# Attention decode kernel: scores computed transposed into PSUM quadrants, with one full-width exp per piece

## The chip, the core and the metric

The kernel runs on one core of a Trainium2 chip. The metric is the time of one execution on the device, in microseconds. The median of the kernel before is 693.8 us. Each time is that of whole executions; the traces are of one profiled execution each. "Before" and "the changed kernel" are the two kernels. A "group" is eight tiles of 128 keys (1024 keys), the unit in which the kernels work, and there are 64 groups in a head. A "head" is one of the 8 key/value heads, each shared by 4 query heads.

The views of the profile that are quoted: the page's groups (instructions by line, engine, operation and shape), the windows (busy time of each engine in stretches of time), the timeline, the DMA queues, and the chain of waits. Engines: PE is the tensor engine, PEld its weight loads, DVE the vector engine, ACT the scalar engine, POOL GpSimd, SP the engine that issues the large DMA transfers.

## The reference

One token goes through an adaLN block with grouped-query attention against a long cache, then a SwiGLU feed-forward block. What takes the time is the attention:

```python
# x: (1, 1, 512), k_cache and v_cache: (1, 8, 65536, 128), all bfloat16
q = (h @ wq).reshape(B, 1, 32, 128).transpose(0, 2, 1, 3)
k = jnp.repeat(k_cache, 4, axis=1)
v = jnp.repeat(v_cache, 4, axis=1)
scores = jnp.einsum('bhqd,bhkd->bhqk', q, k) * 128 ** (-0.5)
p = softmax(scores, axis=-1)
o = jnp.einsum('bhqk,bhkd->bhqd', p, v)
```

The two caches are 2 x 8 x 65536 x 128 x 2 bytes = 268.4 MB. Each byte is read once. The weights add 17 MB.

## The kernel before

All operations go through a small scheduler that puts in the semaphore waits; each engine runs its own operations in program order. The parts that the change and the argument touch (cuts are marked):

```python
NKB = 4; NVB = 4        # K and V buffers of one chunk (2 MB = 8 groups) each
RT = 8; NB = 3; DT = 3  # ring of transposed K; PSUM banks; T runs 3 groups ahead
LV = OPH + LAT          # PV runs 64 + 8 groups behind the scores

dma("sp", "ld_x", xT_bf, x_col, ...)   # 512 pieces of 2 bytes
dma("sp", "ld_c", cT_bf, c_col, ...)   # 512 pieces of 2 bytes
dma("sp", "ld_wmod", ...)              # 3 MB, then wq (4 MB), then K chunks
# ... adaLN, layer norm, q ... then per group o:
def T_op(o):     # PE: 4 transposes of 128x128 fp32 (pairs of bf16) into a PSUM bank
def evac_op(o):  # DVE (ACT for every fourth): that bank -> ring[o % RT]
def S_op(o):
    for pi_ in range(4):
        pair = ring[r][...].rearrange("p (s two) -> p s two", two=2)
        for par in range(2):
            e.matmul(sps[:, sbank, REP*tl:REP*tl + 64], lhsT=pair[:, :, par],
                     rhs=M64[:, g, par, :, :], start=(par == 0), stop=(par == 1))
def bank_ops(o):                        # each 8 groups
    e.tensor_reduce(out=pm4[:, :, k], in_=hview, axis=AX.X, op=ALU.max)   # DVE
    e.tensor_copy(S_sb[gp][:, :, k*BLT:(k+1)*BLT], hview)                 # DVE
def head_softmax_ops(g):                # ACT, 2 pieces x 4 query heads
    e.activation(out=P_sb[gp][:, t0:t1, h], in_=S_sb[gp][:, h, t0:t1], func=ACT.Exp, ...)
def PVU_op(u):                          # each 2 groups: 4 quadrant matmuls
    for j in range(4):
        e.matmul(ops_[32*j:32*j+16, g % 2, 0:512], lhsT=P_sb[...],
                 rhs=vnat[b][:, tl0+4*j:tl0+4*j+4, :], tile_position=(0, 32*j))
# ...
for s in range(NKO + LV):               # main loop, software pipelined
    T_op(s + DT); pump_dma(); evac_op(s + DT)
    S_op(s); ...                        # bank_ops, head_softmax_ops
    PVU_op((s - LV) // 2); pump_dma()   # every second s
```

`pump_dma` issues the next K or V chunk when its buffer's last reader has been issued; the transfer then waits for that reader. In `S_op` the transposed K is the stationary operand, so the scores come out with 128 keys on 128 partitions and 4 query heads along the columns.

## Time and profile before

| | |
|---|---|
| median | 693.8 us (693.62 to 693.9, 4 runs) |
| bytes moved | 286.56 MB |
| rate in the middle of the run | 426 to 427 GB/s |
| PE, DVE, ACT busy in the 80 us of one head | 65 to 69, 40 to 42, 20 to 21 us |

The windows of the kernel before. The columns are: stretch, its length, busy time of each engine with the number of instructions, granted clock, mean busy share of the 16 DMA engines, GB/s.

```profile
...
core 0: us, PE busy (x) PEld busy (x) DVE busy (x) ACT busy (x) POOL busy (x), PEclk, DMA share, GB/s
0.00:20.00 20.00, 3.87 (x100) 3.65 (x100) 3.41 (x17) 1.49 (x2) 4.36 (x24) 1.00 0.79 316
...
40.00:52.00 12.00, 12.00 (x207) 11.81 (x206) 10.33 (x19) 4.86 (x5) 0.00 (x0) 1.00 1.01 424
52.00:70.00 18.00, 18.00 (x310) 17.71 (x309) 15.56 (x26) 6.25 (x7) 0.00 (x0) 1.00 0.99 409
...
420.00:500.00 80.00, 66.32 (x926) 54.56 (x926) 42.00 (x71) 20.39 (x31) 0.48 (x1) 0.96 1.01 427
...
645.00:670.00 25.00, 10.04 (x74) 3.90 (x74) 1.53 (x5) 0.00 (x0) 0.00 (x0) 0.50 0.96 356
...
```

The row 420:500 is one head; the others between 100 and 580 us read the same. The DMA engines are busy all the time and deliver 427 GB/s, while every compute engine has idle time. At 52 to 70 us, where K comes alone because no probabilities exist yet for V, PE is busy without a gap and the rate is 409 GB/s. The start (0:20) and the weights at the end (645:670) are slower.

The groups of the kernel before: busy time in us, mean ns of one, and idle time of the engine before them.

```profile
...
L491 PE MATMUL sps<-M,arena_k 128*128 128x64 bf16 x4096 | 211.6, 197 | 0.0
...
L558 PE MATMUL ops<-arena_v,P_sb 128*16 128x512 bf16 x1024 | 106.5, 428 | 31.7 <-DMA arena_v<-in_A_v_cache_dram 31.4
L525 ACT ACTIVATE P_sb<-S_sb,negm 128x448 bf16<-128x448 f32 x32 | 36.4, 1289 | 0.0
L503 DVE TENSOR_REDUCE pm<-sps 128x4 f32<-128x256 f32 x64 | 26.6, 416 | 2.0 <-PE sps L491 2.0
L510 DVE COPY S_sb<-sps 128x256 f32<-128x256 f32 x64 | 26.5, 414 | 0.0
...
L525 ACT ACTIVATE P_sb<-S_sb,negm 128x64 bf16<-128x64 f32 x32 | 11.5, 428 | 0.3
...
```

Exp takes 1289 ns for 448 columns and 428 ns for 64: 861 ns for 384 columns, or 2.24 ns per column.

The DMA queues of the kernel before (packets, MB, share of the time of 16 engines), and the chain of waits that ended last:

```profile
...
q1 hardware_dynamic: 27528, 285.49, 98.2%
q8 instruction: 61, 1.00, 0.6%
...
```

```profile
...
DMA 70%; PE 23%; SPq 4%; DVE 2%; issue 0%
...
```

Queue q8 is not data: it is the fetch of instructions, by its kind. The table counts its 61 packets against the same 16 DMA engines as K and V. The start of the kernel before, from its timeline:

```profile
...
0.72 0.43 SPq L283 DMA_DIRECT2D xT_bf<-in_A_x_dram  x1
...
1.21 0.49 SPq L283 DMA_DIRECT2D cT_bf<-in_c_dram  x1
...
1.75 0.50 SPq L284 DMA_DIRECT2D arena_v<-in_w_mod_dram  x1
...
5.95 0.17 DVE L362 TENSOR_SCALAR sc_d<-cT_bf 128x4 f32<-128x4 bf16 x1 [4.02 <-DMA cT_bf<-in_c_dram]
...
29.53 3.68 PE L448 MATMUL ktp<-identf,arena_k 128*128 128x128 f32 x16 [0.80 <-DMA arena_k<-in_A_k_cache_dram]
...
```

### The profile page before, as it was taken

How to read it: one execution, taken by the hardware profiler on the slowest of the kernel's cores; microseconds unless marked ns; L12 is line 12 of the kernel's file. 1: busy time of each engine (PE TensorE's matmuls, PEld its weight loads, DVE VectorE, ACT ScalarE, POOL GpSimd, SP SyncE). 2: the span in 40 equal slices, each digit the busy share in tenths (PEclk: the TensorE clock that was granted, in tenths of full speed). 3: DMA queues.
4: the chain of work that ended last, by engine and by line, in shares of the span. 5: the costliest groups of instructions: out<-in, count | busy, mean ns of one | idle time of the engine just before them, and what ended most of it. 6: DMA issues, size and time to landing. Idle time of an engine off the chain costs nothing.

```text
span 691.6 us, 16865 instructions
## 1 busy us (share of the span) xinstructions
PE 543.6 (79%) x7781; PEld 448.5 (65%) x7781; DVE 333.6 (48%) x594; ACT 167.0 (24%) x253; POOL 8.8 (1%) x33
## 2 busy tenths in 40 slices
PE   1599998788887897888988788788887887784345
PEld 1599986666666676677767676666776776661024
DVE  1288865456444554455645545455553564450001
ACT  0033522142112421214212412114211422123000
POOL 2000000000000000000000000000000000000000
PEclk9999999999999999998989999999998999995555
DMA  7999999999999999999999999999999999999996
GB/s 300 427 428 409 422 427 424 426 428 422 430 426 424 428 427 425 427 425 427 425 427 427 426 423 428 427 425 427 425 425 427 425 428 426 425 410 415 417 329 230
DMA packets 27598, 286.56 MB, mean 414 GB/s; under 512 B 3208, under 2 KB 9096, under 8 KB 10632
## 3 DMA queue, kind: packets, MB, share of 16 engines
q1 hardware_dynamic: 27528, 285.49, 98.2%
q8 instruction: 61, 1.00, 0.6%
q14 instruction: 9, 0.07, 0.0%
HBM read 285.48 MB, written 0.00 MB: 413 GB/s over the span
## 4 chain that ended last, share of the span: by engine, by line
DMA 70%; PE 23%; SPq 4%; DVE 2%; issue 0%
DMA arena_k<-in_A_k_cache_dram 44%; DMA arena_v<-in_A_v_cache_dram 24%; PE ktp L448 13%; PE sps L491 5%; SPq L284 4%; PE ops L558 3%; DMA arena_k<-in_B_w_down_dram 3%; DVE arena_k L474 1%; PE misc L573 1%; DVE X_sb L567 1%; DVE pm L503 0%; DVE S_sb L510 0%; PE misc L674 0%; SPq L283 0%; PE misc L515 0%
## 5 line engine op out<-in xcount | busy, mean ns | idle before, releaser
L448 PE MATMUL ktp<-identf,arena_k 128*128 128x128 f32 x2048 | 349.1, 296 | 69.6 <-DMA arena_k<-in_A_k_cache_dram 69.6
L474 DVE COPY arena_k<-ktp 128x512 f32<-128x512 f32 x398 | 275.0, 691 | 258.4 <-PE ktp L448 256.3
L448 PEld LDWEIGHTS ktp<-identf,arena_k 128*128 128x128 f32 x2048 | 229.6, 148 | 126.5 <-issue 67.8
L476 ACT ACTIVATE arena_k<-ktp 128x1024 bf16<-128x1024 bf16 x114 | 116.7, 1024 | 444.1 <-PE ktp L448 444.1
L491 PE MATMUL sps<-M,arena_k 128*128 128x64 bf16 x4096 | 211.6, 197 | 0.0
L491 PEld LDWEIGHTS sps<-M,arena_k 128*128 128x128 bf16 x4096 | 198.8, 101 | 8.2 <-issue 0.2
L558 PE MATMUL ops<-arena_v,P_sb 128*16 128x512 bf16 x1024 | 106.5, 428 | 31.7 <-DMA arena_v<-in_A_v_cache_dram 31.4
L558 PEld LDWEIGHTS ops<-arena_v,P_sb 128*16 128x16 bf16 x1024 | 24.6, 89 | 57.0 <-DMA arena_v<-in_A_v_cache_dram 40.4
L525 ACT ACTIVATE P_sb<-S_sb,negm 128x64 bf16<-128x64 f32 (+1 forms) x64 | 47.1, 858 | 0.3
L503 DVE TENSOR_REDUCE pm<-sps 128x4 f32<-128x256 f32 x64 | 26.6, 416 | 2.0 <-PE sps L491 2.0
L510 DVE COPY S_sb<-sps 128x256 f32<-128x256 f32 x64 | 26.5, 414 | 0.0
L567 DVE COPY X_sb<-ops 128x512 f32<-128x512 f32 x8 | 5.5, 683 | 39.6 <-PE ops L558 39.6
L573 PE MATMUL misc<-sel,X_sb 128*128 128x4 f32 x64 | 9.8, 276 | 11.1 <-DVE X_sb L567 11.1
L573 PEld LDWEIGHTS misc<-sel,X_sb 128*128 128x128 f32 x64 | 9.2, 222 | 14.1 <-issue 5.5
L525 ACT ACTIVATION_READ_ACCUMULATOR P_sb<-S_sb,negm 128x1 f32 x64 | 14.2, 222 | 0.0
L660 ACT ACTIVATE g_e<-g_c 128x14 f32<-128x14 f32 x1 | 0.2, 215 | 56.4 <-DVE g_c L658 56.4
L378 PE MATMUL misc<-sT,arena_v 128*128 128x1 bf16 x96 | 2.7, 165 | 13.5 <-DMA arena_v<-in_w_mod_dram 13.5
L508 POOL CROSS_LANE_REDUCE rmax<-pmax 128x4 f32<-128x4 f32 x8 | 3.9, 484 | 598.9 <-PE sps L491 383.7
L378 PEld LDWEIGHTS misc<-sT,arena_v 128*128 128x128 bf16 x96 | 2.6, 104 | 13.5 <-DMA arena_v<-in_w_mod_dram 13.5
L418 PE MATMUL misc<-hT,arena_v 128*128 128x1 bf16 x128 | 3.6, 165 | 6.2 <-DMA arena_v<-in_A_wq_dram 6.2
L635 PE MATMUL misc<-attnT,arena_k 128*128 128x1 bf16 x128 | 3.6, 165 | 5.7 <-DMA arena_k<-in_A_wo_dram 5.7
L418 PEld LDWEIGHTS misc<-hT,arena_v 128*128 128x128 bf16 x128 | 3.5, 104 | 6.3 <-DMA arena_v<-in_A_wq_dram 6.3
(85 smaller groups left out, 44.9 us busy)
## 6 DMA issues: line engine op xcount, KB each, us to landing
arena_k<-in_A_k_cache_dram SPq DMA_DIRECT2D x64, 2048.0 KB, 31.0
arena_v<-in_A_v_cache_dram SPq DMA_DIRECT2D x64, 2048.0 KB, 31.0
arena_v<-in_A_wq_dram SPq DMA_DIRECT2D x1, 4096.0 KB, 22.3
arena_k<-in_A_wo_dram SPq DMA_DIRECT2D x1, 4096.0 KB, 28.6
arena_v<-in_w_mod_dram SPq DMA_DIRECT2D x1, 3072.0 KB, 11.7
arena_k<-in_B_w_gate_dram SPq DMA_DIRECT2D x1, 1792.0 KB, 32.9
arena_k<-in_B_w_up_dram SPq DMA_DIRECT2D x1, 1792.0 KB, 14.8
arena_k<-in_B_w_down_dram SPq DMA_DIRECT2D x1, 1792.0 KB, 18.2
```

Of the source, the lines that this page charges most:

```text
L284: return [e.dma_start(out_ap, in_ap)]
L418: insts.append(e.matmul(misc[:, 64 + hd:64 + hd + 1], lhsT=wq_sb[:, kt, hd * P:(hd + 1) * P], rhs=hT[:, kt:kt + 1], start=(kt == 0), stop= ...
L448: insts.append(e.transpose(ktp[:, bank, pi_ * P:(pi_ + 1) * P], knat32[b][:, j * 4 + pi_, :], identf[:, :]))
L474: emit = lambda e: [e.tensor_copy(ring32[r], ktp[:, bank, :])]
L476: emit = lambda e: [e.activation(out=ring[r], in_=ktp[:, bank, :].bitcast(BF16), func=ACT.Copy)]
L491: insts.append(e.matmul(sps[:, sbank, REP * tl:REP * tl + 8 * 2 * REP], lhsT=pair[:, :, par], rhs=M64[:, g, par, :, :], start=(par == 0), ...
L503: op("dve", f"bmax{bl}", lambda e: [e.tensor_reduce(out=pm4[:, :, k], in_=hview, axis=AX.X, op=ALU.max)], reads=[("sps", sbank)], writes=[ ...
L510: op("dve", f"bcopy{bl}", lambda e: [e.tensor_copy(S_sb[gp][:, :, k * BLT:(k + 1) * BLT], hview)], reads=[("sps", sbank)], writes=[("S", g ...
L525: return [e.activation(out=P_sb[gp][:, t0:t1, h], in_=S_sb[gp][:, h, t0:t1], func=ACT.Exp, bias=negm[gp][:, h:h + 1], scale=SCALE, accum_o ...
L558: insts.append(e.matmul(ops_[32 * j:32 * j + 16, g % 2, 0:512], lhsT=lhsT, rhs=vnat[b][:, tl0 + 4 * j:tl0 + 4 * j + 4, :], start=first, st ...
L567: op("dve", f"xcopy{g}", lambda e: [e.tensor_copy(X_sb[:, :], ops_[:, g % 2, :])], reads=[("ops", g % 2)], writes=[("X",)])
L573: insts.append(e.matmul(misc[:, 8:8 + REP], lhsT=X_sb[:, tau * P:(tau + 1) * P], rhs=sel[:, tau, :], start=(tau == 0), stop=(tau == 3)))
```

## The change

Intent: make the small query operand the stationary one and stream the transposed K, so that scores come out transposed (query heads on partitions, keys along columns). Four PSUM quadrants hold 8 rows each. A unit of 4 groups then needs 8 matmuls of 512 columns in place of 32 of 64, and exp runs over all heads at once: two ACT instructions per head, with 1024 and 7168 columns, in place of eight. The price: only 32 of 128 partitions carry scores, so exp covers four times the columns; and the probabilities must be turned back for the PV matmul, with a DVE transpose and a compacting copy for every two groups. The PV matmuls are issued in two halves, two quadrants each. In passing, the x and c loads move from the SP to the ACT queue.

```diff
-        dma("sp", "ld_x", xT_bf[:, :], x_col, ...)
-        dma("sp", "ld_c", cT_bf[:, :], c_col, ...)
+        dma("act", "ld_c", cT_bf[:, :], c_col, ...)
+        dma("act", "ld_x", xT_bf[:, :], x_col, ...)
 ...
-        def S_op(o): ...
+        def SU_op(u):                     # each 4 groups
+                for a0 in (0, 2):
+                    for par in range(2):
+                        for a in (a0, a0 + 1):
+                            e.matmul(sps[32*a:32*a + 2*REP, sbank, 0:512], lhsT=M8[:, g, par, :],
+                                     rhs=R4[:, :, 32*a:32*a + 32, par], ..., tile_position=(0, 32*a))
+            op("act", f"scopy{u}", ... S_st[gp][:, uh*512:(uh+1)*512] <- sps[:, sbank, :], func=ACT.Copy)
+        def smax_op(u):                   # DVE, two groups later
+            e.tensor_reduce(out=pmu[:, uh:uh+1], in_=S_st[gp][:, uh*512:(uh+1)*512], axis=AX.X, op=ALU.max)
 ...
-                for h in range(REP):
-                        e.activation(out=P_sb[gp][:, t0:t1, h], in_=S_sb[gp][:, h, t0:t1], func=ACT.Exp, ...)
+                    reg = S_st[gp][:, u0*512:u1*512]
+                    e.activation(out=reg, in_=reg, func=ACT.Exp, bias=negm_p[gp][:, 0:1], scale=SCALE, ...)
+        def PT_op(u):                     # DVE, each 2 groups
+            e.transpose(out=PTraw[wb], in_=S_st[gp][:, wh*256:(wh+1)*256])
+            e.tensor_copy(PT[gp][:, wh*64:(wh+1)*64], PTraw[wb] 8 of every 32 columns)
 ...
-            op("pe", f"PVU{u}", emit, ...)                 # 4 quadrants together
+            if half == 0:
+                op("pe", f"PVU{u}a", lambda e: emit(e, (0, 1)), ...)
+                return
+            op("pe", f"PVU{u}b", lambda e: emit(e, (2, 3)), ...)   # one group later
```

(Cuts marked with "..."; also cut are the mask that picks each head's maximum, zeroing of the score banks, and which fourth evacuation goes to ACT.)

## The prediction

> **What bounds the kernel now.** DMA. The timeline in 40 slices shows DMA at 9 in every slice but the first two-tenths of start-up and 422 to 428 GB/s in nearly all; the windows by head (80 us each, from 100 to 580 us) give DMA share 1.01 and 426 to 427 GB/s, while PE is busy 65 to 69 us of 80, DVE 40 to 42, ACT 20 to 21. The chain of waits is 70% DMA. 286.56 MB at 427 GB/s are 671 us; the other 20 us are start-up (first 20 us at DMA share 0.79) and the tail (645 to 670 us at 356 GB/s, then about 4 us of chain after the last weight lands). The change moves no byte of K, V or weights.
>
> **What the change removes and adds, per head (80 us, 64 groups of eight K tiles).**
> - PE: score matmuls go from 512 with 128-column weights (0.40 us per group, 25.6 us) to 128 of 512 columns in quadrants. Four quadrant PV matmuls of 512 columns take 0.39 us together in the timeline, 1.88 us for 16 at half clock, so a unit of eight in pairs is, as an estimate, 0.9 to 1.7 us per four groups: 14 to 27 us. PE gets lighter or stays.
> - ACT: exp loses 8 instructions (4 x 1.29 and 4 x 0.43 us, plus read-outs, about 7.7 us). It gains 16 copies of 512 columns; the 1024-column copy took 1.02 us, so about 0.6 us each, 9.6 us. The new exp covers 8192 columns, because only 32 of 128 partitions hold scores: four times the columns of before. The old exp cost 2.24 ns per column (1289-428 ns over 384), with a strided bf16 output. The new output is contiguous; the Trainium skill ("ScalarE: Activation LUTs", "What ACT_TABLE_LOAD costs") gives 0.833 ns per element for every function, and the 1024-column copy agrees. So 1.1 + 6.2 = 7.3 us. ACT about 30 of 80 us.
> - DVE: loses 8 x (0.416 + 0.414) = 6.6 us. It gains 16 maxima of 512 columns (416 ns for 256 columns, so about 0.68, 11 us), 32 transposes of 256 columns (estimate 0.42 us at the copy's rate; 13.5 us) and 32 small copies (0.2 us; 6.4 us). DVE about 66 of 80 us, the new busiest engine, still under the DMA's pace.
>
> **New waits.** The score copy after the long exp waits for it on ACT, and the maximum of that unit blocks DVE, so evacuations and transposes stall about 4 to 6 us once per head. K/V loads take 31 us from issue to landing at 4.9 us a chunk, so about six are in flight; the stall thins that queue and doesn't drain it.
>
> **What reaches the critical path.** The x and c loads leave the SP queue, so the first large load issues at about 0.7 instead of 1.75 us: 1 us gained. At 52 to 70 us, where only K streams, PE was 100% busy and DMA fell to 409 GB/s; there DVE (0.52+0.17 us per group) now takes PE's place: from 1 us gained to 1.5 lost. The tail is V and weight DMA; extra small operations hide under the 5.7 us wait for wo.
>
> **Prediction: 692.8 us, 690.5 to 697.0.** Faster by over 2%: 0.01; within 2%: 0.94; slower by over 2%: 0.05.
>
> **Right if** the windows per head still show 425 GB/s or more, with DVE 60 to 70, PE under 65, ACT 27 to 33 of 80 us; the groups show the 7168-column exp near 6.2 us and the transpose near 0.4. **Wrong if** the transposes or exp run at 2 ns per column or slower: then DVE or ACT stalls drain the load queue, DMA share falls below 0.97 in mid-kernel and the time goes to 710 or more.

## More of the kernel before

The c load lands before 6 us, and the first K transpose runs at 29.53 us, as soon as K is there.

## The result, and the profile after

The changed kernel has a median of 691.07 us (690.22 to 692.11, 9 runs) against 693.83 us (13 runs of before). The ratio is 0.9959, 95% interval 0.995 to 0.9969. Ratios here are the mean time of one kernel's fast runs over that of the other's fast runs of the same rounds, so not quite the ratio of the medians that are quoted. The gain of 2.8 us is small but clear of noise. Later the same kernel gave 692.13 us and 0.9976 (after_again, below).

The windows of the changed kernel, for the stretches shown of before and with the same columns:

```profile
...
0.00:20.00 20.00, 2.70 (x96) 2.64 (x96) 2.79 (x9) 1.49 (x2) 5.38 (x32) 1.00 0.92 339
...
40.00:52.00 12.00, 12.00 (x113) 8.04 (x111) 11.49 (x20) 7.54 (x10) 0.00 (x0) 1.00 0.96 371
52.00:70.00 18.00, 18.00 (x168) 12.55 (x167) 17.10 (x29) 11.25 (x14) 0.00 (x0) 1.00 1.00 404
...
420.00:500.00 80.00, 72.51 (x539) 38.28 (x537) 62.91 (x141) 32.27 (x36) 0.48 (x1) 0.94 1.01 427
...
645.00:670.00 25.00, 8.91 (x66) 3.55 (x58) 2.29 (x9) 0.00 (x0) 0.00 (x0) 0.50 1.02 374
...
```

In the row of one head, DMA still runs at 427 GB/s. DVE went from 42 to 63 us, and PE went up instead of down, from 66 to 73 us. At 40 to 52 us there is a hole that before did not have: 371 GB/s with DMA share 0.96.

The groups that are new or changed:

```profile
...
L590 PE MATMUL ops<-arena_v,PT 128*16 128x512 bf16 x1024 | 193.6, 426 | 54.6 <-DVE PT L566 40.5 <-DMA arena_v<-in_A_v_cache_dram 10.8 <-DVE PTraw L564 3.1
...
L564 DVE STREAM_TRANSPOSE PTraw<-S_st 128x256 bf16<-128x256 bf16 x256 | 111.3, 435 | 1.4 <-ACT S_st L547 1.4
L524 DVE TENSOR_REDUCE pmu<-S_st 128x1 f32<-128x512 bf16 x128 | 86.6, 677 | 40.0 <-ACT S_st L517 40.0
L512 PE MATMUL sps<-arena_k,M 128*8 128x512 bf16 x1024 | 83.0, 395 | 0.3 <-DVE arena_k L486 0.3
L517 ACT ACTIVATE S_st<-sps 128x512 bf16<-128x512 f32 x128 | 75.5, 595 | 54.5 <-PE sps L512 52.3
L547 ACT ACTIVATE S_st<-S_st,negm_p 128x7168 bf16<-128x7168 bf16 x8 | 50.0, 6253 | 0.0
L566 DVE COPY PT<-PTraw 128x64 bf16<-128x64 bf16 x256 | 46.8, 183 | 8.9
...
```

The one long exp takes 6253 ns for 7168 columns. The score matmuls fell from 211.6 to 83.0 us, and the PV matmuls went from 106.5 to 193.6 us although they are the same 1024 matmuls.

The DMA queues and the chain of waits of the changed kernel:

```profile
...
q8 instruction: 37, 0.61, 0.4%
q14 instruction: 14, 0.11, 0.0%
...
```

```profile
...
PE 50%; DMA 25%; DVE 10%; ACT 10%; SPq 4%; issue 1%; POOL 0%; ACTq 0%; DVEq 0%
...
```

The instruction queue q8 carries 37 packets in place of 61. (A second one, q14, carries 14 smaller ones, 8 KB each, in place of 9.) The chain now names PE first with 50%, though the DMA engines are as busy as before. The experiments show what to make of that.

The start of the changed kernel, from its timeline:

```profile
...
0.72 0.48 ACTq L290 DMA_DIRECT2D cT_bf<-in_c_dram  x1
...
0.73 0.45 SPq L291 DMA_DIRECT2D arena_v<-in_w_mod_dram  x1
...
1.23 0.59 ACTq L290 DMA_DIRECT2D xT_bf<-in_A_x_dram  x1
...
13.00 0.17 DVE L379 TENSOR_SCALAR sc_d<-cT_bf 128x4 f32<-128x4 bf16 x1 [5.64 <-DMA cT_bf<-in_c_dram]
...
25.09 0.17 DVE L389 CAST xT<-xT_bf 128x4 f32<-128x4 bf16 x1 [11.07 <-DMA xT_bf<-in_A_x_dram]
...
32.90 3.44 PE L460 MATMUL ktp<-identf,arena_k 128*128 128x128 f32 x15
...
```

The first large load is issued at 0.73 instead of 1.75 us. But c is used only at 13.00 us and x at 25.09 us, since they land that late. The layer norm, q and the first K transpose wait for them, and K starts at 32.90 instead of 29.53 us.

To see where time is gained and lost, take every data packet of the trace and ask when the first N megabytes had landed. The table gives the lag behind the kernel before, in us; negative is ahead. (The bytes of K, V and weights are the same in all of these kernels, and x and c add 2 KB, so equal N is equal progress. This table is worked out from the traces' packets, for one profiled execution each; that of the changed kernel took 690.26 us, near the fast end of its runs. Times count from the start of the trace; counted from the start of the span, a whole column shifts by up to 0.4 us, while the differences down a column stay.)

| MB landed | changed | changed, again | small loads back | before, small loads moved | more waits on PE | rows |
|---|---|---|---|---|---|---|
| 5 | -1.22 | -1.37 | 0.13 | -1.61 | -0.01 | -2.30 |
| 14 | -1.05 | -1.28 | 0.19 | -1.51 | 0.01 | -2.43 |
| 24 | 1.12 | 2.31 | -0.02 | 1.28 | -0.10 | -2.39 |
| 34 | 0.17 | 1.65 | -0.84 | 1.17 | -0.96 | -3.46 |
| 60 | 0.10 | 1.44 | -1.05 | 1.33 | -0.84 | -3.50 |
| 250 | -1.23 | 0.07 | -2.33 | 1.30 | -1.54 | -4.77 |
| 285.4 | -3.34 | -1.82 | -3.78 | 1.69 | -2.22 | -6.32 |

For the changed kernel the column reads: 1.1 us ahead after the start, 2.2 us lost between 14 and 24 MB (about 40 to 65 us), 1.0 us regained by 34 MB, then a slow, steady gain of 1.3 us up to 250 MB, then 2.1 us at the end. In the second profiled execution (692.13 us) the loss between 14 and 24 MB is 3.6 us and the other parts are similar. So a small net result is the sum of several parts; of these the prediction had named the first and, as a range around zero, the one in the phase where K comes alone.

### The profile page after: what moved, and what is told of

The parts are those of the page before. It is cut to its first block, busy times and chain, and to the rows that moved or that the text cites. A ratio compares the mean times of both kernels' runs of the same rounds, so it can differ in the third digit from the quotient of the medians.

```text
span 688.5 us, 11328 instructions
## 1 busy us (share of the span) xinstructions
PE 570.4 (83%) x4709; PEld 315.5 (46%) x4709; DVE 497.9 (72%) x1132; ACT 253.3 (37%) x277; POOL 10.4 (2%) x42
## 4 chain that ended last, share of the span: by engine, by line
PE 50%; DMA 25%; DVE 10%; ACT 10%; SPq 4%; issue 1%; POOL 0%; ACTq 0%; DVEq 0%
PE ktp L460 29%; DMA arena_k<-in_A_k_cache_dram 15%; PE ops L590 11%; ACT S_st L547 9%; PE sps L512 7%; DMA arena_v<-in_A_v_cache_dram 4%; DVE arena_k L486 4%; SPq L291 4%; DMA xT_bf<-in_A_x_dram 3%; DMA arena_k<-in_B_w_down_dram 3%; DVE PTraw L564 2%; PE misc L606 2%; DVE pmu L524 2%; ACT S_st L517 1%; DVE PT L566 1%
## 5 line engine op out<-in xcount | busy, mean ns | idle before, releaser
L460 PE MATMUL ktp<-identf,arena_k 128*128 128x128 f32 x2048 | 339.2, 294 | 15.0 <-DMA arena_k<-in_A_k_cache_dram 8.0
L590 PE MATMUL ops<-arena_v,PT 128*16 128x512 bf16 x1024 | 193.6, 426 | 54.6 <-DVE PT L566 40.5
L488 ACT ACTIVATE arena_k<-ktp 128x1024 bf16<-128x1024 bf16 x114 | 116.8, 1024 | 276.9 <-PE ktp L460 276.9
L524 DVE TENSOR_REDUCE pmu<-S_st 128x1 f32<-128x512 bf16 x128 | 86.6, 677 | 40.0 <-ACT S_st L517 40.0
L564 DVE STREAM_TRANSPOSE PTraw<-S_st 128x256 bf16<-128x256 bf16 x256 | 111.3, 435 | 1.4 <-ACT S_st L547 1.4
L590 PEld LDWEIGHTS ops<-arena_v,PT 128*16 128x16 bf16 x1024 | 43.3, 89 | 143.1 <-DVE PT L566 49.9
L517 ACT ACTIVATE S_st<-sps 128x512 bf16<-128x512 f32 x128 | 75.5, 595 | 54.5 <-PE sps L512 52.3
L512 PE MATMUL sps<-arena_k,M 128*8 128x512 bf16 x1024 | 83.0, 395 | 0.3 <-DVE arena_k L486 0.3
L547 ACT ACTIVATE S_st<-S_st,negm_p 128x1024 bf16<-128x1024 bf16 (+1 forms) x16 | 59.2, 3701 | 33.4 <-DVE negm_p L542 33.4
L566 DVE COPY PT<-PTraw 128x64 bf16<-128x64 bf16 x256 | 46.8, 183 | 8.9
L512 PEld LDWEIGHTS sps<-arena_k,M 128*8 128x8 bf16 x1024 | 13.7, 83 | 22.7 <-issue 22.3
L606 PEld LDWEIGHTS misc<-sel,X_sb 128*128 128x128 f32 x64 | 14.2, 327 | 11.3 <-DVE X_sb L600 11.3
## 6 DMA issues: line engine op xcount, KB each, us to landing
arena_k<-in_A_k_cache_dram SPq DMA_DIRECT2D x64, 2048.0 KB, 25.2
arena_v<-in_w_mod_dram SPq DMA_DIRECT2D x1, 3072.0 KB, 11.3
```

The source lines that it names most:

```text
L460: insts.append(e.transpose(ktp[:, bank, pi_ * P:(pi_ + 1) * P], knat32[b][:, j * 4 + pi_, :], identf[:, :]))
L488: emit = lambda e: [e.activation(out=ring[r], in_=ktp[:, bank, :].bitcast(BF16), func=ACT.Copy)]
L512: insts.append(e.matmul(sps[32 * a:32 * a + 2 * REP, sbank, 0:512], lhsT=M8[:, g, par, :], rhs=R4[:, :, 32 * a:32 * a + 32, par], start=(p ...
L517: op("act", f"scopy{u}", lambda e: [e.activation(out=S_st[gp][:, uh * 512:(uh + 1) * 512], in_=sps[:, sbank, :], func=ACT.Copy)], reads=[( ...
L524: op("dve", f"smax{u}", lambda e: [e.tensor_reduce(out=pmu[:, uh:uh + 1], in_=S_st[gp][:, uh * 512:(uh + 1) * 512], axis=AX.X, op=ALU.max) ...
L547: return [e.activation(out=reg, in_=reg, func=ACT.Exp, bias=negm_p[gp][:, 0:1], scale=SCALE, accum_out=lpart[:, g, pi:pi + 1])]
```

## The experiments

Twelve kernels ran, on three chips, each beside fresh runs of the kernel before (medians 693.64, 693.54 and 693.77 us). All twelve gave correct results.

| run | median us | range us | ratio to before, 95% interval |
|---|---|---|---|
| after_again | 692.13 | 690.83 to 692.78 | 0.9976 (0.9964 to 0.9988) |
| small_loads_back | 690.13 | 689.98 to 690.18 | 0.9949 (0.9937 to 0.9961) |
| before_small_loads_moved | 697.07 | 695.27 to 698.54 | 1.005 (1.0038 to 1.0062) |
| after_more_instructions | 749.51 | 748.14 to 750.08 | 1.0802 (1.0789 to 1.0816) |
| more_waits_on_pe | 690.70 | 690.64 to 690.98 | 0.996 (0.9947 to 0.9972) |
| more_waits_on_pe_double | 797.05 | 796.22 to 798.58 | 1.1492 (1.1475 to 1.1509) |
| pv_whole | 690.00 | 689.91 to 690.1 | 0.9949 (0.9936 to 0.9961) |
| long_stall_1 | 722.61 | 721.0 to 723.51 | 1.0421 (1.0403 to 1.0438) |
| long_stall_2 | 770.61 | 770.1 to 771.16 | 1.1109 (1.1092 to 1.1126) |
| long_stall_1_pv_whole | 690.45 | 690.31 to 690.83 | 0.9954 (0.9939 to 0.9969) |
| rows | 687.36 | 687.2 to 687.42 | 0.991 (0.9897 to 0.9924) |
| rows_pv_whole | 687.25 | 687.1 to 687.55 | 0.9907 (0.9892 to 0.9922) |

### 1. The start: is moving the small loads a gain?

The changed kernel as it is, as a yardstick:

> The changed kernel as it is, so that the other runs of this call have a yardstick from the same chip. Expected: 0.996 of the kernel before (about 691.0 us), within 0.1%.

It gave 692.13 us, 1 us more than expected, with a spread of 2 us.

Then the part undone:

```diff
-        dma("act", "ld_c", cT_bf[:, :], c_col, ...)
-        dma("act", "ld_x", xT_bf[:, :], x_col, ...)
+        dma("sp", "ld_x", xT_bf[:, :], x_col, ...)
+        dma("sp", "ld_c", cT_bf[:, :], c_col, ...)
```

> The changed kernel with the x and c loads back on the SP queue ahead of the large ones, as before the change. Theory (start-up is a trade): the early issue of the large loads brings data 1.1 us sooner, but x and c then land at 13 and 25 us instead of 3.5 and 6 us, the first K transpose starts at 32.9 instead of 29.5 us, K buffers come free later and the load rate falls to 371 GB/s at 40 to 52 us, which costs about 2.2 us of load time. So this run should start K near 29.5 us, keep 420 GB/s or more at 40 to 52 us and be 0.5 to 1.5 us FASTER than the changed kernel (689.5 to 690.5 us). Rival (the early issue is a plain gain, as the prediction said): 1 us SLOWER than the changed kernel, about 692 us.

And the part alone, in the kernel before (the reverse edit):

> The kernel before, with that part of the change alone: x and c loads on the ACT queue. Trade theory: K starts about 3.4 us later, the load rate dips at 40 to 55 us, and since this kernel's K-only phase is slower (0.70 against 0.65 us per group of eight tiles) the lost time isn't regained: 0.5 to 2 us SLOWER than the kernel before (694.3 to 696). Rival (plain gain): 1 us faster, 692.8 us.

The rows of the windows of small_loads_back, then of before_small_loads_moved:

```profile
...
40.00:52.00 12.00, 12.00 (x113) 8.04 (x112) 11.49 (x20) 7.58 (x10) 0.00 (x0) 1.00 1.00 423
52.00:70.00 18.00, 18.00 (x168) 12.50 (x166) 17.11 (x29) 11.25 (x14) 0.00 (x0) 1.00 1.01 430
...
```

```profile
...
40.00:52.00 12.00, 12.00 (x213) 11.81 (x210) 10.33 (x18) 4.47 (x5) 0.00 (x0) 1.00 0.99 376
52.00:70.00 18.00, 18.00 (x311) 17.72 (x308) 15.56 (x26) 6.14 (x6) 0.00 (x0) 1.00 0.98 375
...
```

With the small loads back on SP, K starts at 29.45 us, the hole is gone (423 and 430 GB/s), and the kernel is 2.0 us faster than the changed kernel of the same call (0.5 to 1.5 us had been expected). The part alone makes the kernel before 3.4 us slower by the medians, more than the 0.5 to 2 us that was expected, with 376 and 375 GB/s in these rows. Both directions agree: the rival, a plain gain of 1 us, falls. How a late start becomes a hole shows in the waits of the SP queue: until the first transposes are done, no K buffer comes free for the next load. SP waits up to 11.3 us for the transposes at this point in the changed kernel and up to 7.4 us in small_loads_back (`--waits --engine SP --window 25:70`). The spread is telling as well: the kernels that load x and c as 2-byte pieces on the ACT queue vary by 1.9 to 3.3 us from run to run. With the pieces on SP, small_loads_back varies by 0.2 us, and the kernel before by 0.6 to 1.0 us.

Why do the small loads land late? The Trainium skill ("DMA: Bandwidth & Descriptors", "Queues, rings and completion order") says that SP and ACT each own one row of rings on the same 16 DMA engines, and that an engine takes turns between the rows that have work, packet by packet. On SP the small loads stand ahead of the large ones in the same ring; on ACT they take turns with them. The trace agrees: the 1024 pieces of 2 bytes, 64 per engine, spread over 20.6 us. Those of c came 0.28 us apart on an engine, beside 6 KB packets that took 0.28 us on average, and those of x 0.36 us apart, beside 8 KB packets that took 0.31 us. A piece itself takes 0.009 us.

### 2. Removing the cause instead of moving it

```diff
-        dma("act", "ld_c", cT_bf[:, :], c_col, ...)      # 512 pieces of 2 bytes, x the same
+        dma("act", "ld_c", c_rows[:, :], c_row, ...)     # 4 rows of 256 bytes, x the same
+        op("pe", "cx_tr", lambda e: [
+            e.matmul(misc[:, 300:304], lhsT=c_rows[:, :], rhs=ident[0:4, 0:4], start=True, stop=True),
+            e.matmul(misc[:, 304:308], lhsT=x_rows[:, :], rhs=ident[0:4, 0:4], start=True, stop=True)], ...)
+        # two small DVE copies: misc -> cT_bf, xT_bf
```

> The changed kernel with x and c loaded as 4 rows of 256 bytes on the ACT queue (8 packets in all) and turned by two small matmuls, in place of 1024 packets of 2 bytes. Theory: it keeps the early issue of the large loads (1.1 us) and loses the late landing: x and c land before 5 us, K starts at 28.5 to 29 us, no dip at 40 to 52 us; 1 to 1.8 us faster than with the loads back on SP: 688.3 to 689.2. Rival (the late landing was not what cost time): no better than 690.1.

The windows of rows:

```profile
...
0.00:20.00 20.00, 4.08 (x102) 3.77 (x102) 4.65 (x22) 1.49 (x2) 5.93 (x33) 1.00 0.92 366
...
40.00:52.00 12.00, 12.00 (x114) 8.34 (x114) 11.36 (x19) 7.67 (x10) 0.00 (x0) 1.00 1.02 431
52.00:70.00 18.00, 18.00 (x169) 12.46 (x167) 17.11 (x29) 11.34 (x14) 0.00 (x0) 1.00 1.00 425
...
```

It gave 687.36 us, 6.2 us faster than before and better than expected. K starts at 27.21 us. The start is 2.3 us ahead of before (366 against 316 GB/s in the first 20 us) instead of 1.1 us: the pieces of 2 bytes cost not only their own landing, but also time on the DMA engines for the others. The packets show where: in both the changed kernel and rows the first packet of the 3 MB load starts 1.8 us into the span, but its last packet ends at 11.6 us in the changed kernel and at 10.6 us in rows. So 1.0 of the further 1.2 us is lost while the pieces take turns with that load. The gain over small_loads_back is 2.8 us (1 to 1.8 us had been expected); the run shows it for the whole edit.

### 3. The steady gain: instruction fetch

Between 60 and 250 MB the changed kernel gains 1.3 us at an even pace. The Trainium skill ("Runtime: NRT & Kernel Launch", "Instruction fetch mechanics") says that a sequencer streams its instructions in blocks of 16 KB, which is 256 instructions, through its own DMA queue. The trace agrees to the packet for q8, if that queue serves PE alone: before, 2 x 7781 PE and PEld instructions are 60.8 blocks, and q8 shows 61; in the changed kernel 2 x 4709 are 36.8, and q8 shows 37. A 16 KB instruction packet takes 1.06 us of one engine, so 24 fewer, spread over 16 engines, are an estimated 1.6 us of DMA time over the whole run. Of these packets 40 start between 60 and 250 MB in before and 24 in the changed kernel: 16 fewer, an estimated 1.06 us of the 1.3. The page calls the cost of such a boundary "mostly hidden".

The first test put memsets on POOL:

```diff
+            op("pool", f"fill{s}", lambda e, s=s: [e.memset(scr[:, s*22+i_:s*22+i_+1], 0) for i_ in range(22)], ...)
```

> The changed kernel with 11264 one-byte memsets more on the otherwise idle POOL engine. Fetch theory: the steady gain of about 1.3 us between 160 and 600 us of the changed kernel comes from 5537 fewer instructions, whose fetch takes DMA time (61 against 37 packets of 16 KB, 1.07 us each, over 16 engines: 1.6 us less). 11264 more should bring about 44 more packets and cost 2.5 to 3.5 us against the changed kernel: about 694 us. Rival (the gain comes from the lighter PE or the quicker engines, the fetch is hidden): no change, within 0.5 us.

It came to 749.51 us instead of 694. The memsets were fetched, but through the other queue: q8 stayed at 37, while q14 rose from 14 to 102 packets, 88 more of 8 KB, one for each 128 memsets. What that cost can't be read off, since the memsets slowed the compute. Its queue and its groups:

```profile
...
q14 instruction: 102, 0.84, 0.3%
...
L487 DVE COPY arena_k<-ktp 128x512 f32<-128x512 f32 x398 | 326.9, 912 | 74.1 <-PE ktp L461 67.4
...
L567 DVE COPY PT<-PTraw 128x64 bf16<-128x64 bf16 x256 | 170.3, 665 | 9.8
...
```

The compacting copies went from 183 to 665 ns and the evacuations from 690 to 912 ns, while the transposes stayed near their 435 ns (458). The Trainium skill ("SBUF — State Buffer", "SBUF: two separate sides") says that POOL and some DVE operations take an exclusive lock on a shared port pair; the run agrees that POOL work that shares no data with DVE slows it. That the lock is the cause is not shown. An idle engine was not a free place.

The second test put satisfied semaphore waits into the PE stream, on the base of small_loads_back:

```diff
+                op("pe", f"fill{s}", lambda e: [e.wait_ge(eng_sem["dve"], 1) for _ in range(11)])
```

> Base of this call: the changed kernel with the x and c loads back on SP (690.1 us). This run adds 5632 satisfied semaphore waits to the PE instruction stream, about as many instructions as the change took away (5537)[...]. Fetch theory: about 22 more instruction packets of 16 KB and 1.2 to 1.8 us more than the base: 691.3 to 692. Rival (fetch is hidden; the steady gain comes from lighter engines): 690.1, within 0.3 us.

The instruction queue of more_waits_on_pe:

```profile
...
q8 instruction: 48, 0.79, 0.5%
...
```

It gave 690.70 us, less than the 691.3 to 692 us that were expected: 0.57 us more than its base, and 0.70 us more than pv_whole (below), which is as fast as the base. The profile counts 2801 more instructions and not 5632, and 11 more packets, an estimated 11 x 1.06 / 16 = 0.73 us. In the table above it falls behind small_loads_back by 0.58 us between 60 and 250 MB, with its groups running at the same 4.08 us per four in mid-head. In that stretch it has 8 packets more (31 against 23), so by its own slope the 16 of the change are 0.58 / 8 x 16 = 1.2 us, close to the 1.3 us to be explained. But the dose is not clean: between 34 and 60 MB it loses 0.3 us with no packet more, and after 250 MB another 0.8 us with 1 more (379 against 407 GB/s at 612 to 627 us). So the waits cost time in some other way too, and part of the 0.58 us may be of that kind.

> The earlier run put 5632 waits into the source, but the profile counts only 2801 more instructions than its base and 11 more instruction packets (48 against 37); it cost 0.57 us. This run doubles the dose: about 5600 more instructions, as many as the change took away, 22 more packets. Fetch theory: the cost doubles, 1.0 to 1.4 us against the base with the x and c loads back on SP (690.1): 691.1 to 691.5. Rival (the 0.57 us was something else about these waits): no clear doubling.

This came to 797.05 us. The packets were there (59), but so many waits slow PE itself, so that the load rate falls to 360 GB/s on average. It can't tell fetch from PE time and doubles nothing. Further support comes from the other kernels: before and before_small_loads_moved have the same 61 packets, and their distance stays put between 60 and 250 MB (1.33 and 1.30). The runs with 37 packets gain 1.3 to 1.4 us there, whether PE is busier (changed) or lighter (pv_whole, 1.3 us). So the lighter or busier PE is not the cause, and fetch is the best explanation of the steady gain. It is supported by one dose of half the size that has side effects, and it is not proven: in all these kernels the packets change together with the rest of the attention code.

### 4. Why PE got busier, and whether it matters

```diff
-            if half == 0:
-                op("pe", f"PVU{u}a", lambda e: emit(e, (0, 1)), ...); return
-            op("pe", f"PVU{u}b", lambda e: emit(e, (2, 3)), ...)
+            if half == 0:
+                op("pe", f"PVU{u}", lambda e: emit(e), ...); return      # all four quadrants
```

> Base as above, with the four quadrant PV matmuls of a unit issued together again instead of two and two. Theory: the prediction missed that halves don't overlap as four do (0.39 us for two, 0.39 us for four), which is why PE busy is 71 to 73 of 80 us per head and not under 65. PE busy should fall by 8 to 13 us per head; the time stays within 0.5 us of 690.1 because DMA binds. Rival: PE is a co-limit (it was 50% of the chain of waits), and the time falls by 1 us or more.

The windows of pv_whole for one head, and its PV group:

```profile
...
420.00:500.00 80.00, 60.68 (x542) 36.44 (x538) 61.12 (x142) 32.22 (x36) 0.48 (x1) 0.94 1.01 427
...
```

```profile
...
L590 PE MATMUL ops<-arena_v,PT 128*16 128x512 bf16 x1024 | 110.3, 436 | 81.0 <-DVE PT L566 51.2 <-DMA arena_v<-in_A_v_cache_dram 26.5 <-DVE arena_k L486 2.7
...
```

PE falls to 61 us in this head (61 to 63 in the six that were read), PV matmuls to 110.3 us, and the time stays: 690.00 against 690.13 us of small_loads_back (kernels before differ by as much: 693.54 and 693.64). So two quadrant matmuls take as long as four (0.39 us in the timelines), and halving the unit had doubled the cost. And although the chain of waits gave PE 50%, taking 10 us of PE out of each head was worth nothing that can be measured. The chain followed one of two processes that run side by side at nearly the same pace (77 and 79 us per head, as the next section works out).

### 5. How far is compute from binding?

The timeline of the changed kernel at the start of a head shows the stall that the prediction expected:

```profile
...
232.74 6.25 ACT L547 ACTIVATE S_st<-S_st,negm_p 128x7168 bf16<-128x7168 bf16 x1
...
239.60 0.69 DVE L524 TENSOR_REDUCE pmu<-S_st 128x1 f32<-128x512 bf16 x1 [4.91 <-ACT S_st L517]
...
```

The long exp holds ACT, the score copy queues behind it, and DVE waits 4.91 us for that copy before its next maximum; PE waits for DVE. To test how much of this the load queue absorbs, dummy copies lengthen the time on ACT:

```diff
+                if pi == NPIECE - 1:
+                    for r_ in range(2):      # 1 in long_stall_1
+                        op("act", f"dwell{g}_{r_}", lambda e: [e.activation(out=reg, in_=reg, func=ACT.Copy)], ...)
```

> Base as above, with two dummy ACT copies of 7168 columns before the long exp of each head: 12.4 us more ACT time in the place where VectorE waits 4.9 us, as if exp cost 2.6 ns per column. The prediction called 2 ns or slower fatal (710 us or more). Rule to test: the time per head is the larger of 80 us (DMA) and VectorE's busy 63 us plus the stall; 63 + 17.3 = 80.3, so 690 to 696 us. Rival (the prediction's words: the stall drains the load queue): 710 or more.

It came to 770.61 us, so the rule under test (VectorE's busy time plus the stall) falls. Its steady groups run at 4.07 us per four, 1.02 us each, the same 4.08 us per four as small_loads_back shows in mid-head: DVE evacuates a bank, PE transposes the next group, runs its half of the PV matmuls, and hands back. Neither engine is full; the pace is that of the hand-offs. 64 groups at that pace are 65 us, and the stall and the change from head to head come on top. DMA needs 33.55 MB / 427 GB/s = 78.6 us per head.

> Base: the changed kernel with the x and c loads back on SP. One dummy copy of 7168 columns before the long exp: 6.2 us more per head, as if exp cost 1.7 ns per column. The run with two copies came to 770.6 us and refuted the rule 63 us busy plus stall: its groups ran at 4.07 us per four, 65 us per head, and its heads took about 90 us, so without the copies a head needs about 77.6 us of compute against about 79 us of DMA. Margin theory: 2 us of the 6.2 are hidden, the rest shows in seven to eight heads: 718 to 730 us. Rival (the slack is larger and two copies crossed a cliff): under 700 us.

722.61 us, as expected. Both doses, counted against the 690.13 us of small_loads_back, give the same margin: (770.61 - 690.13) / 8 heads = 10.1 us of 12.3 us (two copies of 6.17 us) show, and (722.61 - 690.13) / 8 = 4.1 of 6.2. About 2.1 to 2.3 us per head are hidden. The starts of the long exp show the same without the division by 8: from the second head to the seventh they follow each other every 79.0 us in small_loads_back, 83.2 us with one copy and 89.4 us with two. Less the copies, both give about 77.1 us of compute per head, about 2 us under the loads. That is all the room the changed kernel has.

> As long_stall_1, but with the four quadrant PV matmuls issued together. If the pace of a group (1.02 us) is set by PE and its hand-offs with VectorE, then the 10 us per head of PE time that this saves widens the margin, and most of the extra stall is hidden: 690 to 705 us. If the pace is set by VectorE alone: as long_stall_1, within 5 us.

The window of one head, long_stall_1 and then long_stall_1_pv_whole:

```profile
...
420.00:500.00 80.00, 71.08 (x522) 37.85 (x522) 61.48 (x136) 33.30 (x34) 0.48 (x1) 0.91 0.96 401
...
```

```profile
...
420.00:500.00 80.00, 60.84 (x538) 37.21 (x536) 59.55 (x139) 37.95 (x36) 0.48 (x1) 0.87 1.01 427
...
```

With the PV matmuls whole, the same longer stall costs nothing: 690.45 against 722.61 us. Four groups then take 3.52 us, as its timeline shows, with DVE at work nearly all the time. So PE's share of the hand-off sets the pace in the changed kernel, and an estimated 9 us per head (64 groups at 0.88 instead of 1.02 us) become margin. Of this the run shows the 4 us per head that no longer appear; how much more there is was not tested.

> The best version so far (x and c as rows, 687.4 us) with the PV matmuls issued together. DMA binds, so 687.0 to 687.5 us: no gain over rows alone beyond 0.3 us, but more margin.

687.25 us: no gain over rows beyond noise, as expected, and the fastest version that was run. It beats both kernels.

### What stays open

The last 35 MB bring the changed kernel another 2.1 us, and small_loads_back 1.5 us. A part lies where K ends and V goes on alone. The windows of before, then of the changed kernel:

```profile
...
612.00:627.00 15.00, 11.69 (x170) 8.76 (x168) 6.61 (x13) 5.59 (x14) 0.48 (x1) 0.95 0.97 391
...
```

```profile
...
612.00:627.00 15.00, 11.52 (x84) 5.54 (x83) 10.97 (x32) 7.36 (x7) 0.48 (x1) 0.80 1.00 419
...
```

15 us at 28 GB/s more are 15 x 28 / 427 = 1.0 us; small_loads_back has 407 GB/s there, only 0.6 us. This is where before waits for its last head's exp, but no run separates that from the score matmuls, which are fewer, and from the phase in which the last chunks fall, so it is an account and not a cause shown. Another 0.9 to 1.0 us comes between 275 and 280 MB, among the last weights, in the changed kernel and in small_loads_back alike; why is open.

## Why the prediction was right or wrong

The time (691.07 us; predicted 692.8, range 690.5 to 697) and "within 2%" were right, and so was the main reason: DMA binds, and the change moves no byte of K, V or weights. 427 GB/s per head was measured. That the time came so close is luck in part: the sum had one term wrong (the start) and lacked two (the fetch and the end), and these largely cancelled. Point by point:

- **"Right if ... DVE 60 to 70 ... ACT 27 to 33":** right. DVE 60.8 to 64.8 and ACT 30.5 to 32.8 us per head.
- **Unit costs:** right. Exp 6.25 us (predicted 6.2), transposes 435 ns (420), maxima 677 ns (680), copies 183 ns (200), score copies 595 ns (600). The Trainium skill ("ScalarE: Activation LUTs", "What ACT_TABLE_LOAD costs") gives 280 ns plus 0.833 ns per column for an instruction with a pointer bias, from which the estimate for 7168 columns is 6251 ns; 6253 was measured. The column rate of before (2.24 ns) did not carry over to the contiguous output.
- **"the maximum of that unit blocks DVE ... 4 to 6 us once per head ... thins that queue and doesn't drain it":** right. 4.91 us at the head shown (40.0 us over the eight), and the DMA share stayed at 1.01. The median time from issue to landing of a K chunk fell from 31.0 to 25.2 us, so fewer loads are in flight; that the stall alone does this is not shown.
- **"PE gets lighter or stays", "PE under 65":** wrong. 70 to 73 us. The step that failed counted only the score matmuls and missed that the change splits the PV matmuls into halves, which do not overlap as four do. pv_whole shows 61 to 63.
- **"the first large load issues at about 0.7 instead of 1.75 us: 1 us gained":** right for the first 14 MB (1.1 us) and wrong as a term of the sum. The same line delays x and c, which delays K by 3.4 us and loses 2.2 us of load time (3.6 in the second profiled execution). Net, the line cost 2.0 us in the changed kernel and 3.4 us in the kernel before.
- **"from 1 us gained to 1.5 lost" in the K-only phase:** without the late start it is a gain of about 0.9 us (small_loads_back at 34 MB, and 430 against 409 GB/s at 52 to 70 us).
- **Missing:** about 1.3 us of steady gain, most likely instruction fetch, whose packets stand in the queue table of the kernel before, and the 2.1 us at the end, of which "The tail is V and weight DMA" foresaw nothing. These outweighed the loss at the start, which is why the total came out 1.7 us below the forecast.
- **"DVE about 66 of 80 us ... still under the DMA's pace":** true, but it reads as 14 us of room and there were about 2. Busy time adds up what an engine does, not what it waits for in the hand-off with PE.
- **"Wrong if ... exp run at 2 ns per column or slower ... 710 or more":** the direction was right and the threshold too high. 1.7 ns per column (long_stall_1) already gives 722.6 us.

## What to carry to other kernels

In this kernel, which is bound by its loads, a restructuring of compute moved the time at the edges (start, end, the phase where K comes alone) and, most likely, by the DMA time of its own instructions, so cost those; and look at incidental lines, since moving two tiny loads to another queue took back 2.0 of the 3.5 us that the rest of the change won. How much compute room is left is not read from busy shares but from the pace of a group in a stretch where it runs freely, times the number of groups, plus the stalls; a deliberate delay on the chip measures it directly. Here issuing the quadrant matmuls all four together gave margin, and turning loads of 2-byte pieces into rows gave 2.8 us.

## What the Trainium skill lacked or had wrong

- "Runtime: NRT & Kernel Launch", "Instruction fetch mechanics" calls the fetch "mostly hidden". Here the blocks are counted on the DMA engines that carry the data: 1.06 us of one engine per 16 KB block, against 0.62 us for a 16 KB data packet. A run with 11 blocks more was 0.57 us slower, though not all of this need be fetch. The page gives 16 KB as the size of a block; 11264 memsets on POOL came in 88 packets of 8 KB.
- "DMA: Bandwidth & Descriptors", "Queues, rings and completion order" gives a turn as a packet of some 9 to 17 descriptors. As worked out above, the pieces of 2 bytes got about one per turn here, each beside one packet of the large loads: 0.28 to 0.36 us between them on an engine. So a load of 512 pieces took 12.3 us (c) and 23.8 us (x) from issue to landing beside a stream of large packets, against 4.7 and 2.8 us ahead of it in the same queue.
- "Perfetto Trace Analysis", "Identifying the Most-Contended Engine" judges DVE and ACT by occupancy. Here DVE at 63 of 80 us and PE at 73 left only about 2 us of room, because of the hand-offs between them. No page describes measuring the room by a deliberate delay.
